# Three w_in blocks in four by seven products instead of eight, halves of w_in and w_out in turn, and an order from a planner

## The chip, the cores and the metric

The kernel runs on one core of one Trainium2 chip. The metric is the device time of one execution in microseconds (us); lower is better.

## What is computed

Attention with a soft cap on the scores, and behind it two feed-forward layers on the 896 tokens (batch 2 of 448, model width 768, inner width 2048). The reference, cut to what matters:

```
scores = cap * tanh(q @ k.T / 8 / cap)            # 2 x 12 heads, 448 x 448, head width 64
x  = softmax(scores) @ v                          # heads side by side: 896 x 768
h  = x @ w_in          # 768 -> 2048              first layer
x  = (s * relu(h)**2 + b) @ w_out                 # 2048 -> 768
h  = x @ w2_in         # 768 -> 2048              second layer
out = (h * clip(h + 3, 0, 6) / 6) @ w2_out        # 2048 -> 768
```

The four weight matrices reach the device as 64-bit words that hold each value in double format. The kernel makes float32 of them itself.

## The kernel before

**Precision.** Every float32 operand of a feed-forward product is split into two parts that TensorE multiplies in its fp32r format: `hi` is the value cast to fp32r, `lo` is the value minus `hi`. A product of a 128x128 weight block with a 128x448 operand block (448 tokens, one batch) is then three matmuls (lo·hi, hi·lo, hi·hi) into one PSUM bank. I call these three a piece. `products` (line 101) issues a piece.

**Tiling.** With KD = 6 blocks of 128 in the model width and KF = 16 in the inner width, each layer has 16 w_in chunks `f`, each of 6 pieces for each of the two batches (36 matmuls), and then 6 output blocks `mt`, each of 16 pieces for each batch, whose weights come in three chunks of 6, 6 and 4 blocks. That is 1152 matmuls a layer, 2304 in all, all recorded at line 104.

**A weight chunk's way.** SyncE's queue loads the raw 64-bit words of a chunk (`fetch`, line 54; up to 768 KB, three buffers `raw`). ScalarE rescales the upper halves (line 68). VectorE shifts them left by 3 (line 80), joins the sign bit (line 82) and joins the three top bits of the lower half (line 84). Then ScalarE casts `hi` (line 93) and VectorE subtracts `lo` (line 99).

**After the products.** `after_in` (line 106) makes the activation of a w_in chunk, once per batch: in the first layer Relu on ScalarE (110), square and scale on VectorE (114), `hi` on ScalarE (121), `lo` on VectorE (128). In the second layer VectorE has one instruction more (116, 117 and 130). `after_out` (132) splits the output into the next layer's operand, or copies it to `y` and stores it.

**Order.** In `iteration` (145) the code issues a piece and then one or more side steps of the chunks that come next (`beside`, 152), so order is what stands in the code: chunk after chunk, all 16 w_in chunks of a layer, then all of w_out.

**Attention.** It runs ahead of this, in 42 units of scores, tanh, exp and attend. Its last steps overlap with the first 18 pieces of the first layer (three chunks, first batch).

Of the kernel before, what the change touches and what calls it, by code (L numbers as in the profile page):

```python
# [9 lines left out]
U32 = mybir.dt.uint32  # L10
I32 = mybir.dt.int32
# [11 lines left out]
CH = 6  # L23
WARM = (S, S, S // 4)
SCALE = 1.0 / D**0.5
FIRST = 3


@with_exitstack
def attention_moe_moe(ctx: ExitStack, tc: tile.TileContext, qk, v, cap, w1i, w1o, s, b, w2i, w2o, out):  # L30
    nc = tc.nc
    const = ctx.enter_context(tc.tile_pool(name="const", bufs=1))
    act = ctx.enter_context(tc.tile_pool(name="act", bufs=1))
    wp = ctx.enter_context(tc.tile_pool(name="wp", bufs=3))
    tp = ctx.enter_context(tc.tile_pool(name="tp", bufs=4))
# [6 lines left out]
    zeros = tp.tile([128, S], F32, name="zeros", tag="h")  # L42
    ones = const.tile([128, D], F32, name="ones")
    x = [[act.tile([128, KD, S], F32R, name=f"x{p}{bi}") for p in ("h", "l")] for bi in range(B)]
    g = {(bi, f): [act.tile([128, S], F32R, name=f"g{p}{bi}{f}") for p in ("h", "l")] for bi in range(1) for f in range(FIRST)}

    chunks = [(w1i[f], 0, KD) for f in range(KF)]
    cuts = [(k, min(k + CH, KF)) for k in range(0, KF, CH)]
    chunks += [(w1o[m], *c) for m in range(KD) for c in cuts]
    chunks += [(w2i[f], 0, KD) for f in range(KF)]  # L50
    chunks += [(w2o[m], *c) for m in range(KD) for c in cuts]
    raws, whole, ready = {}, {}, {}

    def fetch(i):
        if i < len(chunks):
            src, k0, k1 = chunks[i]
            raws[i] = wp.tile([128, CH * 128, 2], U32, name="raw", tag="raw")
            nc.sync.dma_start(raws[i][:, :(k1 - k0) * 128, :], src[:, k0:k1, :].bitcast(U32).rearrange("p k (m t) -> p (k m) t", t=2))

    def rescale(i, dve=False):  # L60

        if i < len(chunks):
            n = (chunks[i][2] - chunks[i][1]) * 128
            up = raws[i][:, :n, 1].bitcast(F32)
            if dve:
                nc.vector.tensor_scalar(up, up, 2.0**-112, None, op0=ALU.mult)
            else:
                nc.scalar.activation(up, up, AF.Copy, scale=2.0**-112)  # L68

    def join(i, step):  # L70

        if i >= len(chunks):
            return
        n = (chunks[i][2] - chunks[i][1]) * 128
        if step == 0:
            whole[i] = wp.tile([128, CH * 128], F32, name="w", tag="w", bufs=2)
        bits = whole[i][:, :n].bitcast(U32)
        up, low = raws[i][:, :n, 1], raws[i][:, :n, 0]
        if step == 0:
            nc.vector.tensor_scalar(bits, up, 3, None, op0=ALU.logical_shift_left)  # L80
        elif step == 1:
            nc.vector.scalar_tensor_tensor(out=bits, in0=up, scalar=0x80000000, in1=bits, op0=ALU.bitwise_and, op1=ALU.bitwise_or)  # L82
        else:
            nc.vector.scalar_tensor_tensor(out=bits, in0=low, scalar=29, in1=bits,  # L84
                                           op0=ALU.logical_shift_right, op1=ALU.bitwise_or)
            raws.pop(i)
            fetch(i + 3)

    def upper(i, dve=False):
        if i < len(chunks):  # L90
            n = (chunks[i][2] - chunks[i][1]) * 128
            ready[i] = [wp.tile([128, CH * 128], F32R, name=f"w{p}", tag=f"w{p}") for p in ("hi", "lo")]
            (nc.vector.tensor_copy if dve else nc.scalar.copy)(ready[i][0][:, :n], whole[i][:, :n])  # L93

    def lower(i):
        if i < len(chunks):
            n = (chunks[i][2] - chunks[i][1]) * 128
            hi, lo = ready[i]
# [65 lines left out]
    def ffn():  # L164
# [23 lines left out]
        for _ in after:  # L188
            pass
# [256 lines left out]
```

## Time and profile before

| | |
|---|---|
| three runs | 566.32, 567.35, 575.05 us; median 567.35 |
| span of the profiled execution, first to last instruction | 565.5 us |
| TensorE busy in it | 559.1 us, 99% |
| VectorE, ScalarE busy in it | 376.9 us (67%), 261.3 us (46%) |

The span is the time that the profile's views divide up. A whole execution has a little more around it: the median run stands 1.85 us above the span, and the fastest 0.8 us. A time for the changed kernel is formed on the span, and the 1.85 us are added again.

### The profile page before, as it was taken

The page shows a single profiled execution, that of the slowest core. Times are in us where ns is not written, and L with a number is a line of the kernel's source. Part 1 is how long each engine was busy: PE and PEld are TensorE (multiplying, and loading weights), DVE is VectorE, ACT ScalarE, POOL GpSimd, SP SyncE. Part 2 cuts the span into 40 slices and gives each one's busy share as a digit, 9 for nine tenths or more (in the row PEclk, how much of TensorE's full clock was granted, in tenths as well). Part 3 has the DMA queues.
Part 4 walks back from the last instruction along what each step waited for, and adds up shares of the span by engine and source line. Part 5 has one row for each costly group of instructions (what it writes and reads, how often), then busy time and mean ns, then how long its engine had stood idle before and what let it go on. Part 6 is the DMA issues. An engine that isn't in the chain of part 4 may idle for free.

```text
span 565.5 us, 6988 instructions
## 1 busy us (share of the span) xinstructions
PE 559.1 (99%) x2790; PEld 459.5 (81%) x2790; DVE 376.9 (67%) x523; ACT 261.3 (46%) x376; POOL 0.4 (0%) x5
## 2 busy tenths in 40 slices
PE   8999999999999999999999999999999999999997
PEld 3223235799999999999999999999999999999996
DVE  2689887899777787545644568888888844544420
ACT  6999992455444443322222235544444532321210
POOL 0000000000000000000000000000000000000000
PEclk9999999999999999999999999999999999999999
DMA  8833411053333233224233413333332335333100
GB/s 318 311 123 121 147 35 34 0 165 115 112 114 111 94 111 119 81 100 150 93 94 112 168 56 112 111 112 111 113 111 83 105 134 159 125 126 127 55 33 34
DMA packets 15131, 64.13 MB, mean 113 GB/s; under 512 B 2022, under 2 KB 3962, under 8 KB 14970
## 3 DMA queue, kind: packets, MB, share of 16 engines
q1 hardware_dynamic: 14952, 63.52, 33.6%
q8 instruction: 22, 0.36, 0.3%
q10 hardware_dynamic: 146, 0.16, 0.1%
q14 instruction: 11, 0.09, 0.1%
HBM read 60.88 MB, written 2.79 MB: 113 GB/s over the span
## 4 chain that ended last, share of the span: by engine, by line
PE 95%; ACT 3%; issue 1%; DVE 1%
PE pf L104 82%; PE ps L222 5%; PE pav L248 4%; ACT t L230 2%; PE pav L245 1%; ACT t L235 1%; PE pz L267 1%; PE pz L336 1%; PE ps L226 1%; PE pz L275 1%; DVE xu L307 0%; DVE xl L312 0%; PE pz L293 0%; PE pz L290 0%; PE pf L290 0%
## 5 line engine op out<-in xcount | busy, mean ns | idle before, releaser
L104 PE MATMUL pf<-xh,wlo 128*128 128x448 f32 x384 | 140.7, 366 | 0.0
L104 PE MATMUL pf<-xl,whi 128*128 128x448 f32 x384 | 140.4, 366 | 0.3 <-DVE xl L312 0.3
L104 PE MATMUL pf<-xh,whi 128*128 128x448 f32 x384 | 140.3, 365 | 0.0
L104 PE MATMUL pf<-gl,whi 128*128 128x448 f32 x384 | 140.2, 365 | 0.0
L104 PE MATMUL pf<-gh,wlo 128*128 128x448 f32 x384 | 140.2, 365 | 0.0
L104 PE MATMUL pf<-gh,whi 128*128 128x448 f32 x384 | 140.2, 365 | 0.0
L93 ACT CAST whi<-w 128x768 fp32r<-128x768 f32 (+1 forms) x67 | 53.4, 797 | 166.3 <-PE pf L104 96.8
L99 DVE TENSOR_TENSOR wlo<-w,whi 128x768 fp32r<-128x768 f32 (+1 forms) x68 | 61.7, 907 | 83.7 <-ACT whi L93 83.7
L104 PEld LDWEIGHTS pf<-xh,wlo 128*128 128x128 f32 x384 | 72.1, 188 | 8.5 <-issue 2.1
L104 PEld LDWEIGHTS pf<-xl,whi 128*128 128x128 f32 x384 | 72.1, 188 | 6.4 <-DVE xl L312 0.7
L104 PEld LDWEIGHTS pf<-xh,whi 128*128 128x128 f32 x384 | 72.1, 188 | 5.7
L104 PEld LDWEIGHTS pf<-gl,whi 128*128 128x128 f32 x384 | 72.1, 188 | 5.7
L104 PEld LDWEIGHTS pf<-gh,wlo 128*128 128x128 f32 x384 | 72.1, 188 | 5.7
L104 PEld LDWEIGHTS pf<-gh,whi 128*128 128x128 f32 x384 | 72.1, 188 | 5.7
L82 DVE SCALAR_TENSOR_TENSOR w<-raw,w 128x768 uint32<-128x768 uint32 (+1 forms) x68 | 62.0, 912 | 2.2
L84 DVE SCALAR_TENSOR_TENSOR w<-raw,w 128x768 uint32<-128x768 uint32 (+1 forms) x68 | 61.9, 911 | 2.3
L68 ACT ACTIVATE raw<-raw 128x768 f32<-128x768 f32 (+1 forms) x67 | 58.1, 868 | 0.0
L230 ACT ACTIVATE t<-ps 128x896 f32<-128x896 f32 x42 | 37.9, 902 | 6.5 <-PE ps L222 6.5
L235 ACT ACTIVATE t<-t 128x896 f32<-128x896 f32 x42 | 39.9, 950 | 1.2
L80 DVE TENSOR_SCALAR w<-raw 128x768 uint32<-128x768 uint32 (+1 forms) x68 | 36.0, 530 | 0.0
L222 PE MATMUL ps<-rqk 64*128 64x448 f32 x144 | 34.8, 586 | 0.6 <-ACT t L230 0.5
L110 ACT ACTIVATE h<-pf,three 128x448 f32<-128x448 f32 x32 | 20.2, 632 | 27.9 <-PE pf L104 27.9
(56 smaller groups left out, 330.1 us busy)
## 6 DMA issues: line engine op xcount, KB each, us to landing
raw<-in_w1i SPq DMA_DIRECT2D x16, 768.0 KB, 4.1
raw<-in_w2i SPq DMA_DIRECT2D x16, 768.0 KB, 4.2
raw<-in_w1o SPq DMA_DIRECT2D x12, 768.0 KB, 4.1
raw<-in_w2o SPq DMA_DIRECT2D x12, 768.0 KB, 4.3
rqk<-in_qk SPq DMA_DIRECT2D x11, 448.0 KB, 6.0
raw<-in_w1o SPq DMA_DIRECT2D x6, 512.0 KB, 3.9
raw<-in_w2o SPq DMA_DIRECT2D x6, 512.0 KB
out<-y SPq DMA_DIRECT2D x12, 224.0 KB, 1.9
```

The costliest lines, as they stand in the source:

```text
L68: nc.scalar.activation(up, up, AF.Copy, scale=2.0**-112)
L80: nc.vector.tensor_scalar(bits, up, 3, None, op0=ALU.logical_shift_left)
L82: nc.vector.scalar_tensor_tensor(out=bits, in0=up, scalar=0x80000000, in1=bits, op0=ALU.bitwise_and, op1=ALU.bitwise_or)
L84: nc.vector.scalar_tensor_tensor(out=bits, in0=low, scalar=29, in1=bits, op0=ALU.logical_shift_right, op1=ALU.bitwise_or)
L93: (nc.vector.tensor_copy if dve else nc.scalar.copy)(ready[i][0][:, :n], whole[i][:, :n])
L99: nc.vector.tensor_sub(lo[:, :n], whole.pop(i)[:, :n], hi[:, :n].bitcast(F32))
L104: nc.tensor.matmul(ps[:, :S], w[a][:, sl], rhs[r], start=(k == 0 and i == 0), stop=(k == n_k - 1 and i == 2))
L110: nc.scalar.activation(t, ps[:, :S], AF.Relu, **({"bias": three} if layer else {}))
L222: nc.tensor.matmul(ps[:, j, :S], raw_qk[p][rows, 1, c * 128:(c + 1) * 128], raw_qk[p][rows, 0, :], start=True, stop=True)
L230: nc.scalar.activation(u_t[n], u_ps.pop(n)[:, :, :S], AF.Tanh, scale=icap_r)
L235: nc.scalar.activation(u_t[n], u_t[n], AF.Exp, scale=cap_r)
L248: nc.tensor.matmul(pav[p][(top, end)[j], :S], va[bi][:, d, (2 * (p % 2) + j) * NC + c, :], u_t[n][:, j, :], start=(p % 2 == 0 and c == 0), ...
```

## The change

It has five parts.

1. **Seven products.** Two w_in chunks `f`, `f+1` and the two batches are taken as a 2x2 block product (the 768 of the model width is cut in two, so each product is three pieces). Eight block products become seven by Strassen's method in a form with running sums. Seven operands are needed on either side: A11, A12, A22 and four sums S1 to S4 from the weights (VectorE, 128x384 each), B11, B21, B22 and four sums T1 to T4 from the layer's input. Partial results go from bank to bank: ScalarE copies product 1 into a second bank (`cp`) and product 5 into SBUF (`c5`); VectorE adds product 5 behind product 6 (`d1`) and behind product 7 (`d2`). The first 8 of the first layer's 16 chunks stay as they were (`PLAIN`), so 12 pairs of the 16 are done in this way.
2. **Halves.** Chunks 0 to 7 of w_in come first, then the 8 of the 16 inner blocks of all six output blocks, whose sums go to SBUF (`partial`); then chunks 8 to 15, and the second half of each output block on a bank that ScalarE has filled with the partial sum.
3. **Join on ScalarE.** The upper halves are rescaled into `w`; the three top bits of the lower half are shifted into the lowest byte of the upper half as bytes, by an ACTIVATE on every eighth byte (`low_bits`); VectorE then joins sign and low bits in one instruction (`merge`). For the first three chunks VectorE does the byte step.
4. **Planned order.** Every step of the feed-forward layers is a task with an engine, a cost and the buffers that it uses. `Plan.order` walks through time with these costs and takes, on each engine, the task that is due first and whose inputs and buffers are there; TensorE may take any of the next 36 pieces. The instructions are issued in the order of the planned starts.
5. **Buffers.** Activations and operands take slots of 128x448 (84 in all); weights lie in two groups of 4 blocks of 384 columns (`gA`) and two of 3 (`gB`).

```diff
-CH = 6
+HK = KD // 2
+BL = HK * 128
+CI = KD * 128
+HF = KF // 2
+CO = HF // 2 * 128
+PLAIN = 8
+SLOTS_A, SLOTS_B = 36, 48
+GROUPS = {"gA": 2, "gB": 2}
+OUT_ORDER = (0, 3, 1, 4, 2, 5)
...
-            nc.vector.tensor_scalar(bits, up, 3, None, op0=ALU.logical_shift_left)
-            nc.vector.scalar_tensor_tensor(out=bits, in0=up, scalar=0x80000000, in1=bits, op0=ALU.bitwise_and, op1=ALU.bitwise_or)
-            nc.vector.scalar_tensor_tensor(out=bits, in0=low, scalar=29, in1=bits,
-                                           op0=ALU.logical_shift_right, op1=ALU.bitwise_or)
...
+            nc.scalar.activation(by[:, :, 4], by[:, :, 3], AF.Copy, scale=1.0 / 32.0, bias=-15.5 / 32.0)
...
+        nc.vector.tensor_scalar(bits, bits, 3, None, op0=ALU.logical_shift_left)
...
+        nc.vector.scalar_tensor_tensor(out=bits, in0=up, scalar=0x80000007, in1=bits, op0=ALU.bitwise_and, op1=ALU.bitwise_or)
...
+            a = add("ACT", acts(n), hi, after, [g])
+            c = add("DVE", dve(n), lambda: nc.vector.tensor_sub(g.tile[1][:, at:at + n], cols, g.tile[0][:, at:at + n].bitcast(F32)), [a], [g])
...
+            s1 = add("DVE", dve(BL), lambda: nc.vector.tensor_add(blk(1), blk(4), blk(6)), [ms[1], *old])
+            s2 = add("DVE", dve(BL), lambda: nc.vector.tensor_sub(blk(3), blk(1), blk(0)), [ms[0], s1, *old])
+            s3 = add("DVE", dve(BL), lambda: nc.vector.tensor_sub(blk(5), blk(0), blk(4)), [*ms, *old])
+            s4 = add("DVE", dve(BL), lambda: nc.vector.tensor_sub(blk(7), blk(2), blk(3)), [ms[0], s2, *old])
...
+            ga, ta = parts("gA", flat[:, :4 * BL], 4 * BL, [ms[0], s1, s2], range(4))
+            gb, tb = parts("gB", flat[:, 5 * BL:], 3 * BL, [ms[1], s3, s4], (5, 6, 7))
...
+        def strassen(layer, f, w, ops):
+
+            a, bb, c = new_bank(), new_bank(), new_bank()
+            p1 = product(w["A11"], ops["B11"], a)
+            head = take_pe()
+            cp = add("ACT", acts(S), lambda: nc.scalar.copy(bb.tile[:, :S], a.tile[:, :S]), p1, [a, bb])
+            p5 = product(w["S1"], ops["T1"], c)
+            s5 = res("slot")
+            c5 = add("ACT", acts(S), lambda: nc.scalar.copy(t_of(s5, F32), c.tile[:, :S]), p5, [c, s5])
+            p2 = product(w["A12"], ops["B21"], a, [cp], first=False)
+            p6 = product(w["S2"], ops["T2"], bb, [cp], first=False, seeded=True)
+            mid = take_pe()
+            d1 = add("DVE", dve(S, True), lambda: nc.vector.tensor_add(c.tile[:, :S], bb.tile[:, :S], s5.tile), [*p6, c5], [bb, c, s5], 0.5)
+            p7 = product(w["S3"], ops["T3"], bb, [d1], first=False, seeded=True)
+            s7 = res("slot")
+            d2 = add("DVE", dve(S, True), lambda: nc.vector.tensor_add(t_of(s7, F32), bb.tile[:, :S], s5.tile), [*p7], [bb, s5, s7], 0.5)
+            p3 = product(w["S4"], ops["B22"], c, [d1], first=False)
+            p4 = product(w["A22"], ops["T4"], bb, [d2], first=False, seeded=True)
+            tail = take_pe()
...
+                head, mid, next_tail = strassen(layer, f, w, ops)
+                pe.extend(head + tail + mid)
+                tail = next_tail
+            pe.extend(tail)
```

In the order that the built programs have, VectorE's row of one w_in chunk in the first layer of the kernel before reads like this (`h` and `gl` are activations, `w` a weight chunk, `wlo` its lower part):

```order
L114 SCALAR_TENSOR_TENSOR h<-h,st 128x448 x2
L80 TENSOR_SCALAR w<-raw 128x768
L82 SCALAR_TENSOR_TENSOR w<-raw,w 128x768
L84 SCALAR_TENSOR_TENSOR w<-raw,w 128x768
L128 SCALAR_TENSOR_TENSOR gl_827<-h,bt,gh_826 128x448
L128 SCALAR_TENSOR_TENSOR gl_829<-h,bt,gh_828 128x448
L99 TENSOR_TENSOR wlo<-w,whi 128x768
```

That is one chunk: eight instructions (the first row holds two), in the same order for every chunk.

In the changed kernel VectorE's row in the first layer's pairs reads like this (`sl` is a slot; L626 is `d1`, L629 is `d2`, L520 to L523 are S1 to S4):

```order
L593 SCALAR_TENSOR_TENSOR sl<-sl,bt 128x448 x2
L579 SCALAR_TENSOR_TENSOR sl<-sl,st 128x448
L626 TENSOR_TENSOR pf<-pf,sl 128x448
L222 TENSOR_SCALAR w<-w 128x2x384 x2
L228 SCALAR_TENSOR_TENSOR w<-raw,w 128x2x384 x2
L629 TENSOR_TENSOR sl<-pf,sl 128x448
L520 TENSOR_TENSOR w<-w 128x384
L521 TENSOR_TENSOR w<-w 128x384
L522 TENSOR_TENSOR w<-w 128x384
L523 TENSOR_TENSOR w<-w 128x384
L593 SCALAR_TENSOR_TENSOR sl<-sl,bt 128x448
L579 SCALAR_TENSOR_TENSOR sl<-sl,st 128x448
```

One join step per chunk is gone, four sums per pair are new, and the two bank sums stand among the weight steps of the next pair.

On TensorE of the kernel before, a w_in chunk's second batch follows the first at once, on another bank, and no VectorE step lies between the two (bank `pf_2793` ends, `pf_2853` begins):

```order
L104 MATMUL pf_2793<-xh1_76,wlo_2720 128x448
L104 MATMUL pf_2793<-xl1_77,whi_2719 128x448
L104 MATMUL pf_2793<-xh1_76,whi_2719 128x448
L104 MATMUL pf_2853<-xh0_74,wlo_2781 128x448
L104 MATMUL pf_2853<-xl0_75,whi_2780 128x448
```

In both kernels each line is one matmul of a piece.

On TensorE of the changed kernel, between the first two pairs, product 6 of a pair ends on bank `pav_829`, product 1 of the next pair runs on `pz_830`, and then product 7 goes on upon `pav_829`:

```order
L232 MATMUL pav_829<-sl_1369,gAh_1561 128x448
L232 MATMUL pav_829<-sl_1316,gAh_1561 128x448
L232 MATMUL pz_830<-xh00_72,gAl_1735 128x448
L232 MATMUL pz_830<-xl00_73,gAh_1734 128x448
L232 MATMUL pz_830<-xh00_72,gAh_1734 128x448
L232 MATMUL pz_830<-xh01_74,gAl_1735 128x448
L232 MATMUL pz_830<-xl01_75,gAh_1734 128x448
L232 MATMUL pz_830<-xh01_74,gAh_1734 128x448
L232 MATMUL pz_830<-xh02_76,gAl_1735 128x448
L232 MATMUL pz_830<-xl02_77,gAh_1734 128x448
L232 MATMUL pz_830<-xh02_76,gAh_1734 128x448
L232 MATMUL pav_829<-sl_1383,gBl_1670 128x448
```

Nine matmuls of another product stand between product 6 and product 7, which needs `d1`. In the last pair of a half of the second layer no next pair is left. There the row of the changed kernel reads like this, product 6 with `gA` and product 7 with `gB`, both on bank `pf_760`:

```order
L232 MATMUL pf_760<-sl_2731,gAl_2965 128x448
L232 MATMUL pf_760<-sl_2748,gAh_2964 128x448
L232 MATMUL pf_760<-sl_2731,gAh_2964 128x448
L232 MATMUL pf_760<-sl_2402,gBl_3031 128x448
L232 MATMUL pf_760<-sl_2429,gBh_3030 128x448
```

Here product 7 follows product 6 with nothing between them.

## Rows read from the trace of the kernel before

**Rows 1.** Page, part 1: busy us of each engine, share of span, instructions.
```profile
PE 559.1 (99%) x2790; PEld 459.5 (81%) x2790; DVE 376.9 (67%) x523; ACT 261.3 (46%) x376; POOL 0.4 (0%) x5
```

**Rows 2.** Chain that ended last, in order of time: start us, us, what.
```profile
107.28 454.86 PE pf L104 x2243
...
562.16 0.53 ACT y L136
```

**Rows 3.** Instruction groups by form, first of six like groups: busy us, mean ns.
```profile
L104 PE MATMUL pf<-xh,wlo 128*128 128x448 f32 x384 | 140.7, 366 | 0.0
```

**Rows 4.** Stretches: us, PE, PEld, DVE, ACT, POOL busy (instructions), PEclk, DMA share, GB/s.
```profile
100.00:150.00 50.00, 49.69 (x244) 44.41 (x241) 44.24 (x62) 26.86 (x45) 0.00 (x0) 1.00 0.28 95
...
400.00:450.00 50.00, 50.00 (x248) 46.34 (x248) 42.83 (x71) 25.54 (x42) 0.00 (x0) 1.00 0.31 103
450.00:500.00 50.00, 50.00 (x249) 46.34 (x248) 24.78 (x34) 13.62 (x20) 0.00 (x0) 1.00 0.44 145
```

**Rows 5.** Page, part 2: granted TensorE clock in 40 slices, tenths of full speed.
```profile
PEclk9999999999999999999999999999999999999999
```

**Rows 6.** Groups by form, VectorE: busy us, mean ns of one.
```profile
L82 DVE SCALAR_TENSOR_TENSOR w<-raw,w 128x768 uint32<-128x768 uint32 x56 | 53.7, 959 | 1.8
...
L99 DVE TENSOR_TENSOR wlo<-w,whi 128x768 fp32r<-128x768 f32 x56 | 53.4, 953 | 65.5 <-ACT whi L93 65.5
...
L80 DVE TENSOR_SCALAR w<-raw 128x768 uint32<-128x768 uint32 x56 | 31.0, 553 | 0.0
L114 DVE SCALAR_TENSOR_TENSOR h<-h,st 128x448 f32<-128x448 f32 x32 | 21.3, 681 | 16.1 <-ACT h L110 16.1
L128 DVE SCALAR_TENSOR_TENSOR gl<-h,bt,gh 128x448 fp32r<-128x448 f32 x32 | 20.3, 678 | 0.0
...
L117 DVE TENSOR_TENSOR h<-pf,h 128x448 f32<-128x448 f32 x32 | 20.0, 625 | 1.1
...
L130 DVE TENSOR_TENSOR gl<-h,gh 128x448 fp32r<-128x448 f32 x32 | 18.5, 618 | 0.0
...
L116 DVE TENSOR_SCALAR h<-h 128x448 f32<-128x448 f32 x32 | 12.5, 390 | 14.8 <-ACT h L110 14.8
...
L99 DVE TENSOR_TENSOR wlo<-w,whi 128x512 fp32r<-128x512 f32 x12 | 8.3, 691 | 18.2 <-ACT whi L93 18.2
```

**Rows 7.** Groups by form, ScalarE: busy us, mean ns of one.
```profile
L68 ACT ACTIVATE raw<-raw 128x768 f32<-128x768 f32 x55 | 50.1, 910 | 0.0
L93 ACT CAST whi<-w 128x768 fp32r<-128x768 f32 x55 | 46.0, 837 | 155.9 <-PE pf L104 96.8 <-DVE w L84 59.0
...
L121 ACT ACTIVATE gh<-h,bt 128x448 fp32r<-128x448 f32 x32 | 19.5, 667 | 0.7 <-DVE h L114 0.7
...
L110 ACT ACTIVATE h<-pf 128x448 f32<-128x448 f32 x32 | 16.8, 541 | 24.9 <-PE pf L104 24.9
...
L93 ACT CAST whi<-w 128x512 fp32r<-128x512 f32 x12 | 7.4, 616 | 10.4 <-DVE w L84 10.4
```

**Rows 8.** VectorE in order of time, from 150 us: start us, us.
```profile
149.99 1.28 DVE L128 SCALAR_TENSOR_TENSOR gl<-h,bt,gh 128x448 fp32r<-128x448 f32 x2
151.19 0.95 DVE L99 TENSOR_TENSOR wlo<-w,whi 128x768 fp32r<-128x768 f32 x1
...
155.42 0.96 DVE L82 SCALAR_TENSOR_TENSOR w<-raw,w 128x768 uint32<-128x768 uint32 x1
156.42 0.96 DVE L84 SCALAR_TENSOR_TENSOR w<-raw,w 128x768 uint32<-128x768 uint32 x1
```

**Rows 9.** TensorE in order of time, around 107 us: a wait for VectorE ends.
```profile
107.28 0.47 PE L104 MATMUL pf<-xl,whi 128*128 128x448 f32 x1 [0.32 <-DVE xl L312]
...
107.59 0.36 PE L104 MATMUL pf<-xh,whi 128*128 128x448 f32 x1
```

**Rows 10.** DMA issues: KB each, median us from issue to landing.
```profile
raw<-in_w1i SPq DMA_DIRECT2D x16, 768.0 KB, 4.1
...
raw<-in_w1o SPq DMA_DIRECT2D x6, 512.0 KB, 3.9
```

More of the change, by code (lines that the diff above doesn't have):

```diff
@@ L10 @@
 U32 = mybir.dt.uint32
+U8 = mybir.dt.uint8
 I32 = mybir.dt.int32
@@ L26, with __init__ @@
 FIRST = 3
+PLAIN = 8
+SLOTS_A, SLOTS_B = 36, 48
+GROUPS = {"gA": 2, "gB": 2}
+OUT_ORDER = (0, 3, 1, 4, 2, 5)
+class Res:
+    def __init__(self, kind, tile=None):
+        self.kind, self.tile, self.left, self.held, self.order = kind, tile, 0, tile is not None, None
+class Task:
+    def __init__(self, engine, cost, run, after, use, number):
+        self.engine, self.cost, self.run, self.use, self.number = engine, cost, run, use, number
+        self.after = list(dict.fromkeys(t for t in after if t is not None))
+        self.then, self.due, self.start, self.end = [], 1e9, None, None
@@ L49, in attention_moe_moe @@
[L49 to L58, printed above, removed]
@@ L89, in upper @@
[L89 to L98, printed above, removed]
-            nc.vector.tensor_sub(lo[:, :n], whole.pop(i)[:, :n], hi[:, :n].bitcast(F32))
@@ L145, in iteration @@
-    def iteration(pieces, side):
-        for j, piece in enumerate(pieces):
-            piece()
-            for one in side[j * len(side) // len(pieces):(j + 1) * len(side) // len(pieces)]:
-                one()
-            yield
-    def beside(i, after):
-        return [lambda: next(after, None), lambda: rescale(i + 3), lambda: next(after, None),
-                lambda: join(i + 2, 0), lambda: join(i + 2, 1), lambda: join(i + 2, 2),
-                lambda: next(after, None), lambda: upper(i + 2), lambda: next(after, None), lambda: lower(i + 2)]
@@ L316, in finish_x, with w_src, early_region, early_fetch @@
         rest_x(p)
+    first_groups, raws = {}, {}
+    def w_src(layer, kind, i):
+        return ((w1i, w1o), (w2i, w2o))[layer][kind][i]
+    def early_region(i):
+        return flat[:, i * CI:(i + 1) * CI]
+    def early_fetch(i):
+        raws[i] = raw_tile()
+        load_raw(raws[i], w1i[i], CI)
+    def early_merge(i):
+        merge(raws[i], CI, early_region(i))
+        if i < FIRST:
+            raws.pop(i)
+            early_fetch(i + 3)
+    def early_upper(i, dve=False):
+        if i % 2 == 0:
+            first_groups[i // 2] = group("gA")
+        hi = first_groups[i // 2][0][:, i % 2 * CI:(i % 2 + 1) * CI]
+        (nc.vector.tensor_copy if dve else nc.scalar.copy)(hi, early_region(i))
@@ new lines, in early_lower, with early_w, first_pieces @@
+    def early_lower(i):
+        hi, lo = (t[:, i % 2 * CI:(i % 2 + 1) * CI] for t in first_groups[i // 2])
+        nc.vector.tensor_sub(lo, early_region(i), hi.bitcast(F32))
+    def early_w(i, k):
+        sl = slice(i % 2 * CI + k * 128, i % 2 * CI + (k + 1) * 128)
+        return [t[:, sl] for t in first_groups[i // 2]]
+    first_ps = []
+    def first_pieces():
+        for f in range(FIRST):
+            ps = psum()
+            first_ps.append(ps)
+            for k in range(KD):
+                matmuls(ps, early_w(f, k), x[0][k], k == 0, k == KD - 1)
+                yield
```

561 lines of the change are left out of this document (442 added, 119 removed).

## The prediction

> **What bounds the kernel now.** I read the page's busy shares first: TensorE is busy for 559.1 of 565.5 us [rows 1]. But a busy matmul here is one whose end is modelled: the groups give 365 to 366 ns for each of the six kinds of matmul [rows 3], and six times 140 us are more than the whole span, so they overlap. What a matmul costs must be read from the chain in order of time: from 107.28 us on it is one piece of 454.86 us with 2243 matmuls and nothing between them [rows 2]. That is 454.86 / 2243 = 0.2028 us for one. Behind it comes only a copy of 0.53 us and the last store. So the feed-forward part is bound by the number of its matmuls alone, and 108 fewer are worth what 108 cost, as long as the other engines keep up. Does a busier VectorE slow the matmuls? The stretches say no: with VectorE at 42.83 us of 50, TensorE starts 248 matmuls, with VectorE at 24.78 it starts 249 [rows 4]. The granted clock is full in every slice [rows 5].
>
> VectorE is the engine to watch: 44.24 us of 50 in the first stretch of the w_in stage [rows 4], 88%.
>
> **The matmuls.** A pair had 2 chunks x 36 = 72; with seven products of three pieces it has 63, and lasts 63 x 0.2028 = 12.8 us in place of 14.6. Twelve pairs save 12 x 9 = 108 matmuls, and the built program has indeed 2196 of them where 2304 stood. 108 x 0.2028 = 21.9 us. Attention, its first 18 pieces and the tail (copy, store) keep their order on every engine but for the join of three chunks, so they stay.
>
> **VectorE beside a pair.** From [rows 6], first layer, per pair: two shifts 2 x 0.553; two merges 2 x 0.958 (I take line 82's price, the same kind and size); S1 to S4 of 384 columns, which no row shows: from 512 and 768 columns (0.691, 0.953) one column costs 1.02 ns, so 0.56 each, 2.24; the lower parts of 1536 and 1152 columns by the same slope 1.74 + 1.35 = 3.09; d1 and d2, two inputs of which one is in PSUM, 2 x 0.625 (line 117); four activations 4 x (0.681 + 0.678) = 5.44. Sum 1.11 + 1.92 + 2.24 + 3.09 + 1.25 + 5.44 = 15.05 us beside 12.8 us of TensorE. In the second layer the activations cost 4 x (0.390 + 0.625 + 0.618) = 6.53, and the sum is 16.1. So VectorE doesn't fit beside a pair. It must borrow from the output blocks, where it has little to do: an output block has 48 matmuls, 9.7 us, and VectorE's two shifts (at most the 0.553 of 768 columns), two merges of 512 (0.69, as the other instruction of that size with two inputs) and one lower part of 1024 (0.691 + 512 x 0.00102 = 1.22) make at most 3.7 us. That is what the halves are for: over a half of the second layer (4 pairs, 6 blocks) VectorE has 4 x 16.1 + 6 x 3.7 = 87 us of work in 109.5 us. In the first layer's second half the new operands add 33 instructions of 0.62: 4 x 15.05 + 22 + 20.5 = 103 in 109.5. It fits if the planner can carry enough across the border. How much it carries I read from the order of the whole program: between the first and the last matmul of a run of four pairs (252 matmuls, 51.1 us) there stand 65 VectorE instructions in the first layer, worth 47.6 us by these rows, then 79 worth 50.9, then 76 worth 48.6. So VectorE is planned at 93 to 100% in three runs. Two things shift that. Instructions that don't need each other overlap: two of 0.68 took 1.20 up to the next start [rows 8], 0.08 less each. Those that do need each other leave 0.04 between them: 155.42 + 0.96, then 156.42 [rows 8]. Together the real need is a few per cent under the sums, so I take it that VectorE keeps up, but with no reserve.
>
> **Where TensorE waits.** Each pair has three hand-overs that the kernel before has not: `cp` (ScalarE) ahead of products 2 and 6, `d1` ahead of 7 and 3, `d2` ahead of 4. In the order nine matmuls, 1.8 us, stand between product 6 and product 7. The hand-over needs the tail of the last matmul (0.36 - 0.20 = 0.16), the sum (0.625), two crossings of 0.04, and the slower start of a matmul that waited (0.47 against 0.36 [rows 9]): 1.0 us. Covered, with 0.8 us to spare, if VectorE has nothing in front. Behind a late `d1` stand the next pair's shifts, merges and the conversion of its weights; TensorE waits for it. At two places, the last pair of each half of the second layer, nothing stands between product 6 and 7: 2 x 1.0 = 2.0 us on the path. For the other hand-overs I bound VectorE's lateness: at nothing, if the overlap above holds, and at 0.7 us for each of the 24 by `d1` and `d2` (two instructions of 0.62 to 0.96 in front, less what is spare), 16.8 us. I take 1.0 us, near the lower end, since the rows leave VectorE just below TensorE's pace. Waits at the output blocks for weights or activations have 7 or more matmuls of cover, most over 30, so nothing.
>
> **ScalarE beside a pair.** Two rescales 2 x 0.910, two byte steps, upper parts of 1536 and 1152 columns (0.86 ns a column from 512 and 768: 1.50 + 1.17), two copies 2 x 0.54, activations 4 x (0.541 + 0.667) [rows 7]. With 0.910 for a byte step, the nearest row (same count, same step of 8 bytes), that is 12.2 us beside 12.8. No row shows bytes: from below 0.837 (contiguous) or even less, from above I take twice the row, 1.82, which adds 1.8 us a pair and, spread over a run that needs 45 of 51 us, costs TensorE some 0 to 6 us in all. I take 0.910, no cost. The 48 copies of partial sums (0.54) stand in the output blocks, where ScalarE has room, and cost nothing.
>
> **Loads.** A half block's load of 512 KB lands 3.9 us after its issue [rows 10]; in the order some ten of 96 rescales stand only 16 to 18 matmuls (3.2 to 3.6 us) behind their issue. ScalarE waits up to 0.7 us there, ahead of weights that TensorE wants 9 matmuls later at the earliest: nothing on the path.
>
> **Sum.** 565.5 - 21.9 + 2.0 + 1.0 = 546.6 us of span; with the 1.85 us around it 548.5 us, 3.3% under the median of 567.35.
>
> **Rivals.** *A, VectorE is late at the hand-overs.* For it: 93 to 100% planned, and a queue in which `d1` stands behind weight steps. Against it: every wait of TensorE also gives VectorE time to catch up. By the upper bound 546.6 + 15.8 + 1.85 = 564 us, no change that can be told (a measurement tells about 2% here: 556.0 or 578.7).
>
> *B, the byte step costs double.* For it: no row has it. 548.5 + 4 = 552.5.
>
> *C, the borrowing fails.* Place: VectorE in the pairs, if groups of weights and slots come free so late that it can work ahead by nothing. Then a pair lasts as long as VectorE needs: 4 x (15.05 - 12.8) + 8 x (16.1 - 12.8) = 35 us, 567.35 - 21.9 + 35 = 580.5, slower. It eats the gain from an average of 1.8 us per pair on, and loses 2% from 2.8. Against it: the order's 47.6 to 50.9 us of VectorE per run.
>
> *D, the clock.* All slices show the full level of 2.4 GHz [rows 5], with pauses of TensorE of 0.32 us [rows 9]. If the new waits let it fall to 1.2 GHz for about one pair behind each of the two uncovered waits, that is 2 x 12.8 = 26 us: 574. The Trainium skill, "TensorE: Matmul & The Clock Gate", section "A second HAM failure mode: psum-queue depth-cycling", says that small idle times between groups of matmuls, where banks are cycled, made the clock swing; the trace of before has such a bank cycle, but no fall, and by that rule the sum would be D's.
>
> That the change doesn't save the matmuls is excluded by the count in the program.
>
> **Chances.** Forecast 0.70 (its own range 545.5, no wait at all, to 552); A 0.13; B 0.08; C 0.06; D 0.03. Faster by over 2%: 0.70 + 0.08 + a share of 0.03 of A (half of its price or less) = 0.81; same: the rest of A and D's part, 0.12; slower: C and a last 0.01, 0.07. The range for 8 in 10 begins at 544.5 (no waits, and 1 us from the shorter join in attention) and reaches up into A as far as 558.
>
> **What would show it.** The chain in time order should show the matmuls of line 232 at 0.203 us each, 2135 of them behind the end of attention, in pieces broken only by VectorE's line 626 at two places. The waits of TensorE for lines 626, 629 and 619 should sum to 2 to 4 us; 17 us would be A. Line 218 with 768 elements should read 0.84 to 0.95 us; 1.8 would be B. VectorE's busy time in a run of pairs should be 90% or more of it with TensorE still at 248 matmuls per 50 us. If a run of four pairs takes 60 us or more, C is right; a clock row below 1.00 is D. The attention part should end within 1 us of 107.

## The result, and the profile after

The changed kernel takes 557.38 us (median of 4, 556.39 to 560.48) beside 566.93 us for the kernel before in the same session (median of 4, 566.32 to 575.05): a ratio of 0.984, interval 0.980 to 0.9885. The prediction was 548.5. The direction is right, but 566.93 - 557.38 = 9.55 us came where 567.35 - 548.5 = 18.85 were forecast. The times of the kernel before cluster at two values, 566 to 567 and 575 to 576; the part on the matmuls' pace gives a reading of this.

The page of the changed kernel answers [rows 1] and [rows 5]: busy us of each engine, share of the span, instructions; then the granted clock in 40 slices.

```profile
span 556.4 us, 7002 instructions
...
PE 543.7 (98%) x2682; PEld 438.4 (79%) x2682; DVE 394.4 (71%) x587; ACT 423.6 (76%) x549; POOL 0.4 (0%) x5
...
PEclk9999999999999999999999999999999999999999
```

TensorE lost its 108 matmuls (2790 to 2682) and the clock is full. ScalarE is the surprise: 423.6 us where it had 261.3. It is now busier than VectorE, which the prediction took for the engine to watch. The span was forecast at 546.6 us and is 556.4, so 9.8 us are to be found.

The chain that ended last, in order of time (start us, us, what), answers [rows 2]:

```profile
158.72 1.35 ACT raw L218
161.98 15.26 PE pf L232 x74
...
223.13 3.59 ACT raw L218 x2
226.74 0.96 DVE w L228
...
308.47 19.84 PE pf L232 x96
...
414.95 9.72 PE pf L232 x48
...
537.83 14.89 PE pf L232 x72
```

Where one piece of 2243 matmuls stood, the chain now leaves TensorE again and again, mostly for line 218, the byte step on ScalarE. And the matmuls have two prices: 9.72 / 48 = 0.2025 us at 415 us, but 19.84 / 96 = 0.2067 at 308 us and 14.89 / 72 = 0.2068 at 538. Worked out from the starts of all line 232 matmuls behind 108.5 us: 21 gaps above 0.23 us hold 8.9 us more than 21 matmuls would, and the others follow each other at 0.2044 us on average (0.2027 before). So of the 9.8 us, 8.9 - 3.0 = 5.9 are waits beyond the 3.0 that were forecast, and 2128 x (0.2044 - 0.2028) = 3.4 are pace, as I call this spacing of matmuls that don't wait. The rest is in the last copy and store, and in rounding.

The waits of TensorE (engine, line, what it waited for; us in total, times, longest):

```profile
PE pf L232 <- ACT sl L587: 2.8, 1, 2.8
PE pf L232 <- DVE pz L626: 1.8, 2, 1.1
PE pf L232 <- DVE sl L593: 0.4, 1, 0.4
PE pav L232 <- DVE gAl L494: 0.3, 1, 0.3
PE pf L232 <- DVE sl L629: 0.2, 1, 0.2
PE pz L232 <- DVE sl L629: 0.2, 1, 0.2
```

This view counts only the engine's idle time. The gaps between starts also hold the tail of the matmul before and the slower start of the one that waited, so they sum to more (8.9 us). The two waits on line 626 (`d1`) are the uncovered hand-overs, forecast at 2 x 1.0. The one of 2.8 us, at the first output block, wasn't forecast. It stands at 161 us, ahead of the first pair by seven products, whose `cp` copy runs at 219 us. The groups by form (busy us, mean ns of one | idle before, releaser) show what is late; they answer [rows 6, 7]:

```profile
L218 ACT ACTIVATE raw<-raw 128x512 uint8<-128x512 uint8 x48 | 62.1, 1388 | 0.2
L218 ACT ACTIVATE raw<-raw 128x768 uint8<-128x768 uint8 x29 | 54.8, 1971 | 0.1
...
L228 DVE SCALAR_TENSOR_TENSOR w<-raw,w 128x512 uint32<-128x512 uint32 x48 | 33.0, 690 | 22.2 <-ACT raw L218 22.1
...
L228 DVE SCALAR_TENSOR_TENSOR w<-raw,w 128x768 uint32<-128x768 uint32 x32 | 30.7, 958 | 24.1 <-ACT raw L218 24.1
...
L494 DVE TENSOR_TENSOR gAl<-w,gAh 128x1536 fp32r<-128x1536 f32 x12 | 21.0, 1753 | 2.5 <-ACT gAh L492 2.5
...
L521 DVE TENSOR_TENSOR w<-w 128x384 f32<-128x384 f32 x12 | 6.7, 557 | 0.3
```

A byte step of 768 columns takes 1.97 us where 0.910 was priced and 1.82 was the upper bound; 512 columns take 1.39. The merges on VectorE wait 22.1 + 24.1 = 46.2 us for it. VectorE's own prices came out as worked out (0.557 for 0.56, 1.753 for 1.74, 0.958 for 0.958).

ScalarE in order of time, ahead of the wait of 2.8 us (start us, us, engine, line, operation):

```profile
153.21 1.35 ACT L218 ACTIVATE raw<-raw 128x512 uint8<-128x512 uint8 x1
...
155.03 1.37 ACT L218 ACTIVATE raw<-raw 128x512 uint8<-128x512 uint8 x1
...
158.72 1.34 ACT L218 ACTIVATE raw<-raw 128x512 uint8<-128x512 uint8 x1
...
160.34 0.66 ACT L587 ACTIVATE sl<-sl,bt 128x448 fp32r<-128x448 f32 x1
```

Line 587 makes the activations that the first output block reads. Byte steps of later output blocks stand in front of it, 1.1 us from one's start to what follows it, and TensorE is idle from 158.3 to 161.05 us.

### The profile page after: what moved, and what is told of

Read it like the earlier page. It is cut to its first block, busy times and chain, and to the rows that moved or that the text cites. A ratio compares the mean times of both kernels' runs of the same rounds, so it can differ in the third digit from the quotient of the medians.

```text
span 556.4 us, 7002 instructions
## 1 busy us (share of the span) xinstructions
PE 543.7 (98%) x2682; PEld 438.4 (79%) x2682; DVE 394.4 (71%) x587; ACT 423.6 (76%) x549; POOL 0.4 (0%) x5
## 4 chain that ended last, share of the span: by engine, by line
PE 71%; ACT 16%; DVE 9%; issue 3%
PE pf L232 31%; PE pav L232 20%; PE pz L232 7%; ACT raw L218 7%; PE ps L265 5%; PE pav L291 4%; ACT w L211 3%; DVE gBl L494 2%; DVE w L228 2%; ACT t L273 2%; ACT gAh L492 1%; PE pav L288 1%; DVE sl L579 1%; ACT t L278 1%; DVE sl L593 1%
## 5 line engine op out<-in xcount | busy, mean ns | idle before, releaser
L232 PE MATMUL pf<-sl,gBh 128*128 128x448 f32 x450 | 128.5, 367 | 0.4 <-DVE sl L593 0.4
L218 ACT ACTIVATE raw<-raw 128x512 uint8<-128x512 uint8 (+1 forms) x77 | 116.9, 1607 | 0.3
L228 DVE SCALAR_TENSOR_TENSOR w<-raw,w 128x512 uint32<-128x512 uint32 (+1 forms) x80 | 63.6, 798 | 46.3 <-ACT raw L218 46.2
L232 PEld LDWEIGHTS pf<-sl,gBh 128*128 128x128 f32 x450 | 84.4, 188 | 8.0 <-DVE sl L593 0.7
L232 PE MATMUL pf<-sl,gBl 128*128 128x448 f32 x225 | 83.0, 369 | 4.9 <-ACT sl L587 2.8
L232 PE MATMUL pav<-sl,gBh 128*128 128x448 f32 x238 | 68.0, 367 | 0.0
L211 ACT ACTIVATE w<-raw 128x512 f32<-128x512 f32 (+1 forms) x79 | 57.9, 763 | 7.6 <-DVE gBl L494 5.4
L232 PE MATMUL pf<-sl,gAh 128*128 128x448 f32 x198 | 56.6, 367 | 0.0
L232 PE MATMUL pav<-sl,gAh 128*128 128x448 f32 x172 | 49.0, 366 | 0.0
L232 PEld LDWEIGHTS pav<-sl,gBh 128*128 128x128 f32 x238 | 44.7, 188 | 4.0
```

The source lines that it names most:

```text
L211: nc.scalar.activation(bits, up, AF.Copy, scale=2.0**-112)
L218: nc.scalar.activation(by[:, :, 4], by[:, :, 3], AF.Copy, scale=1.0 / 32.0, bias=-15.5 / 32.0)
L232: nc.tensor.matmul(ps[:, :S], w[a], rhs[r], start=start and i == 0, stop=stop and i == 2, skip_group_check=True)
```

## Experiments

Theory 1: the byte step, twice as dear as priced, makes ScalarE hand operands over late. Theory 2, rival A of the prediction: VectorE is late at the hand-overs by itself. Theory 3: the rest is a pace of the matmuls that takes one of two values and is drawn anew where TensorE has waited. The sums of waits below are worked out as above, from the starts of the matmuls.

### The byte step made cheap

```
-            nc.scalar.activation(by[:, :, 4], by[:, :, 3], ...)
+            m = {768: 302, 512: 199}[n]
+            nc.scalar.activation(by[:, :m, 4], by[:, :m, 3], ...)
```

> The byte step on ScalarE (line 218) works on 302 of 768 and 199 of 512 columns, all else and the whole order unchanged; the low three bits of the other columns are left out of the weights. Theory 1 (the byte step took 1.39 and 1.97 us where 0.67 and 0.91 were planned, ScalarE ran late, and TensorE's waits of 9 us come from that): line 218 reads about 0.67 and 0.91 us, TensorE's waits fall to 2.5 to 4 us, the time to 548 to 552 us. Theory 2 (VectorE late at the hand-overs d1 and d2, whatever ScalarE does): waits stay at 8 us or more, time 555 to 558. Theory 3 (after a wait the matmuls can fall into a pace of 0.2067 us instead of 0.2027, by chance): with fewer waits fewer stretches at the slower pace, 0 to 4 us of difference between runs.

For the columns that the byte step no longer reaches, the kernel leaves out the low three bits of the weights. 554.42 us median (547.97 to 555.28, 6 runs), ratio 0.9785 [0.9766, 0.9804]; the profiled execution has a span of 547.4. Groups by form, and below them the waits of TensorE in the feed-forward part, line numbers one higher:

```profile
L219 ACT ACTIVATE raw<-raw 128x199 uint8<-128x199 uint8 x48 | 28.1, 680 | 0.2
L219 ACT ACTIVATE raw<-raw 128x302 uint8<-128x302 uint8 x29 | 24.2, 917 | 0.1
```

```profile
PE pf L233 <- DVE pz L627: 1.8, 2, 1.1
```

With the byte step at 0.917 us, the price of the prediction, and every instruction in the same order, only the two uncovered hand-overs are left; the sum of the waits is 2.4 us in place of 8.9. VectorE does the same work (393.0 us), so theory 2 is refuted: VectorE keeps up. ScalarE is busy for 363.9 us, so the dear byte step made up 60 of its 423.6.

In time, 547.97 and 549.18 are the predicted 548.5, but the four others lie about 6 us above. The median misses the 548 to 552 of theory 1, and the spread of 7.3 us the 0 to 4 of theory 3. The profile is of the execution of 549.18, and the granted clock was 0.999 to 1.000 in all six, so the clock isn't the reason; whether the four others lose their time by pace is not shown. By their times alone the two kernels can hardly be told apart (the ratio of the changed one is 0.984 [0.980, 0.9885]). What carries the reading is the waits in the profiles: the one of 2.8 us stands in all three that were taken of the changed kernel's program (one of them with instructions added behind it), and not in this one. The chain shows the output block that took 19.84 us above:

```profile
301.79 19.46 PE pf L233 x96
...
528.88 14.89 PE pf L233 x72
```

19.46 / 96 = 0.2027: the same work at the faster pace, while the end of this execution goes at 0.2068 too.

### What makes the byte step dear

Behind the last block, ten forms of it three times each on 448 columns, for instance:

```
+            nc.scalar.activation(by2[:, :, 4], by[:, :, 3], ...)   # L856
+            nc.scalar.activation(cont[:, :n], by[:, :, 3], ...)    # L858
+            nc.scalar.activation(fl, by[:, :, 3], ...)             # L864
+            nc.scalar.activation(by[:, :, 4], fl, ...)             # L866
```

> The changed kernel, with 30 more instructions behind its last output block, three of each form, on 448 columns: the byte step from and to every eighth byte, to contiguous bytes, from contiguous bytes, both contiguous, from every eighth byte to float32, from float32 to every eighth byte, on 16-bit halves with a step of 8 bytes; the byte and the 16-bit step on VectorE; the byte step on GpSimd. If reading bytes is slow on ScalarE, the forms that read bytes take about 1.25 us and float32 to bytes 0.57; if writing them is slow, bytes to float32 takes 0.57 and the others 1.25; if only the step of 8 bytes is, the contiguous form takes 0.57. On VectorE 1.042 us was seen for 768 columns, so 0.6 to 0.7 for 448. The body before it is a second profile of the changed kernel: theory 3 expects the slower pace in other stretches than in the first.

Groups by form in its last 37 us. The names read alike, so the text says by line which is which:

```profile
L866 ACT ACTIVATE raw<-mf 128x448 uint8<-128x448 f32 x3 | 3.6, 1194 | 0.1
L860 ACT ACTIVATE raw<-raw 128x448 uint8<-128x448 uint8 x3 | 3.6, 1193 | 0.1
L868 ACT ACTIVATE raw<-raw 128x448 uint16<-128x448 uint16 x3 | 3.6, 1193 | 0.1
L856 ACT ACTIVATE raw<-raw 128x448 uint8<-128x448 uint8 x3 | 3.6, 1193 | 7.0 <-DMA raw<-in_w1i 7.0
L874 POOL TENSOR_SCALAR raw<-raw 128x448 uint8<-128x448 uint8 x3 | 3.5, 1180 | 584.8 <-DVE raw L872 584.6
L870 DVE TENSOR_SCALAR raw<-raw 128x448 uint8<-128x448 uint8 x3 | 2.0, 664 | 53.0 <-ACT raw L868 52.9
...
L858 ACT ACTIVATE raw<-raw 128x448 uint8<-128x448 uint8 x3 | 1.8, 597 | 0.1
L864 ACT ACTIVATE mf<-raw 128x448 f32<-128x448 uint8 x3 | 1.8, 594 | 0.1
L862 ACT ACTIVATE raw<-raw 128x448 uint8<-128x448 uint8 x3 | 1.8, 590 | 0.1
```

Reading every eighth byte is free: into contiguous bytes 0.597 us (L858), into floats 0.594 (L864), against 0.590 with both sides contiguous (L862). Writing every eighth byte doubles the time, from bytes (L856, L860), from floats (L866), and with 16-bit elements (L868): the second of the three cases that were named. VectorE does the step in 0.664, GpSimd in 1.180. 16-bit elements without a step were not tried. What runs ahead of the last block is the changed kernel once more; the part on the pace comes back to its profile.

### The planner told the price

```
-            l = add("ACT", acts(n), lambda: low_bits(r.tile, n), ...)
+            l = add("ACT", 0.22 + 0.00228 * n, lambda: low_bits(r.tile, n), ...)
```

> Only a number of the planner is changed: the byte step's cost is 0.22 us + 2.28 ns a column, as measured, instead of 0.19 + 0.85; the work is the same, its order is planned anew. Theory 1: the planner moves the byte steps to where ScalarE has room, the waits fall from 9 us to 3 to 6, time 551 to 554. Theory 2: waits as before, time 556 to 558. If ScalarE has no room left at all, the waits stay but stand where the planner put them.

556.45 us (554.25 to 556.9), ratio 0.980 [0.977, 0.9835]: not to be told from the changed kernel. The waits sum to 7.3 us, and the longest, 1.2 us, is on line 619 of ScalarE:

```profile
PE pf L232 <- ACT pf L619: 2.3, 2, 1.2
```

Waits and time miss what theory 1 expected of this run (3 to 6 us, 551 to 554 us). The wait of 2.8 us is gone, but others came elsewhere: the new order spread the lateness and didn't remove it, which is the third outcome that was named. That ScalarE has no room for the step ahead of the merges fits this, but is not shown by it.

### All pairs by eight products

The pairs of strassen_run take the plain product of eight again; halves, byte join on ScalarE and planner stay.

> All 16 pairs by eight products (2304 matmuls), the other four parts of the change kept: halves, byte join on ScalarE, planner, buffers. Theory 1 and 2: 108 matmuls of 0.2028 us more are 21.9 us, the sums of Strassen's method and the hand-overs are gone, so both engines have room in most stretches; waits only in the first 60 us of the feed-forward part, 3 to 4 us: time 568 to 573, about the kernel before and a little over. If the waits came from the halves or the planner and not from the pairs, it would be 575 or more.

571.52 us median of 566.46, 566.84, 576.19 and 576.67. The kernel before had 566.14 to 567.34 and, twice, 575.55 and 575.96 in the same session, so the two are alike value by value. In the profile no matmul of the feed-forward part waits (no gap above 0.23 us) and all go at 0.2027. Its byte step is as dear (1.955 us for 768 columns, ScalarE 392.6 us busy). So the halves, the byte join and the planned order cost and bring nothing alone, and even the waits of 3 to 4 us that were expected in the first 60 us are absent: the waits need both the dear byte step and what the seven products add. That is not only the shorter pairs with their hand-overs. The waits at 117 and 161 us, 4.3 of the 8.9 us by the gaps, stand ahead of the first pair. There the changed kernel already makes the sums T1 to T4, with five casts of line 442 on ScalarE between 108 and 161 us (2.9 us), one of them right ahead of line 587, and this kernel makes none. Whether those casts alone bring the wait was not tried.

### The byte step on GpSimd, and product 6 first

```
-            nc.scalar.activation(by[:, :, 4], by[:, :, 3], ...)
+            nc.gpsimd.tensor_scalar(by[:, :, 4], by[:, :, 3], 1.0 / 32.0, -15.5 / 32.0, ...)
```

and in a second run, and alone in a third, product 6 ahead of product 2:

```
+            p6 = product(w["S2"], ops["T2"], bb, [cp], first=False, seeded=True)
             p2 = product(w["A12"], ops["B21"], a, [cp], first=False)
-            p6 = product(w["S2"], ops["T2"], bb, [cp], first=False, seeded=True)
```

> The byte step is moved from ScalarE to GpSimd (a multiply-add on the same bytes), and the planner is told its cost there. Theory 1 (ScalarE, slowed by the byte step that takes 1.97 us where 0.91 was priced, hands operands over late): ScalarE falls from 424 to about 300 us busy, the waits of TensorE in the feed-forward part shrink from 9 to 2 to 3 us, and only the two uncovered hand-overs on VectorE's sum d1 (1.8 us together) are left; 548 to 550 us where the matmuls go at 0.2027 us, 553 to 556 where a stretch of them goes at 0.2067. GpSimd's own price should be near 2.0 us for 768 columns (1.18 for 448), 150 us in all. Rival (VectorE is late at the hand-overs by itself): the waits named for VectorE stay, 555 to 558 us. A second rival: GpSimd beside VectorE slows VectorE's instructions; then the merges read more than 0.8 us and the time stays above 556.

> The byte step on GpSimd as in the run before it, and product 6 is asked for before product 2, so that nine matmuls of product 2 stand between product 6 and product 7 everywhere, also in the last pair of a half. If the two waits of 0.9 us on d1 are the uncovered hand-overs, they are gone: 1.8 us less than byte_pool at the same matmul pace, 546 to 548 us at 0.2027 us a matmul and 552 to 554 with a stretch at 0.2067. If the order of products was chosen so because of something else (bank or operand still in use), other waits of the same size take their place and the time is byte_pool's.

> The changed kernel with product 6 before product 2 alone; the byte step stays on ScalarE. Theory 1: the two waits on d1 go (1.8 us), the waits behind the late byte step stay (about 7 us): 554 to 557 us. If VectorE at the hand-overs is the main cause, covering product 7 takes away more than half of the 9 us of waits: 549 to 552.

The first took 595.53 us (ratio 1.051 [1.050, 1.053]), the second 589.64 (1.039 [1.037, 1.041]): far outside what theory 1 expected, by the second rival. Groups by form of the first; line 222, VectorE's shift, takes 423 and 557 ns in the changed kernel:

```profile
L222 DVE TENSOR_SCALAR w<-w 128x512 uint32<-128x512 uint32 x48 | 45.1, 962 | 13.4 <-ACT w L211 13.1
L222 DVE TENSOR_SCALAR w<-w 128x768 uint32<-128x768 uint32 x32 | 40.1, 1264 | 10.0 <-ACT w L211 9.8
```

While GpSimd works, VectorE's shift more than doubles: by the starts and ends in the trace, the 14 shifts of 512 columns that no GpSimd step overlaps take 0.41 us on average, the 34 others 1.19. VectorE's work grows to 469.8 us. So this edit slows another engine and can't speak for or against theory 1. Line 587 then comes 9.8 us late, and the stretches (us, PE, PEld, DVE, ACT, POOL busy, PEclk, DMA share, GB/s) show what this does to the clock:

```profile
155.00:160.00 5.00, 3.40 (x17) 2.81 (x15) 4.58 (x5) 2.40 (x5) 3.95 (x3) 1.00 0.00 0
160.00:165.00 5.00, 0.00 (x0) 0.00 (x0) 2.75 (x5) 2.60 (x4) 1.19 (x1) 0.68 0.68 210
165.00:170.00 5.00, 1.57 (x3) 1.08 (x4) 5.00 (x8) 2.63 (x6) 0.38 (x1) 0.50 0.48 137
170.00:175.00 5.00, 5.00 (x21) 4.52 (x21) 4.96 (x7) 2.11 (x4) 2.73 (x2) 0.80 0.19 76
175.00:180.00 5.00, 5.00 (x27) 4.64 (x26) 4.83 (x9) 2.62 (x4) 0.00 (x0) 1.00 0.54 166
```

The granted clock falls to 0.50, the lower level of 1.2 GHz, and the first whole 5 us behind the wait, from 170 us, hold 21 matmuls, the next 5 us 27.

Product 6 first, alone, gave 556.62 us (554.93 to 558.43), ratio 0.983 [0.980, 0.986], a time as theory 1 expected. The two waits on `d1` are gone as they should be, yet the sum of waits is 9.2 us, not 7: others of 0.5 to 0.7 us on lines 629, 593 and 619 took their place. The lateness moved to other hand-overs; what made those late was not traced. With the byte step on GpSimd the same reordering brought 5.9 us, where 1.8 were expected; why is open.

### Byte steps of w_out on VectorE

Three runs put byte steps of 512 columns on VectorE (0.767 us each) and keep product 6 first: those of layer 2 with the told cost, all 48 with the told cost, all 48 with the old cost.

```
-            l = add("ACT", acts(n), lambda: low_bits(r.tile, n), ...)
+            l = add("DVE" if dve_byte else "ACT", ..., lambda: low_bits(r.tile, n, dve_byte), ...)
```

> Three things at once: the byte step of the 24 w_out blocks of layer 2 on VectorE (a shift of bytes, by the row of 448 columns about 0.74 us for 512), the planner told the measured cost of the byte step on ScalarE (0.22 us plus 2.28 ns a column), and product 6 ahead of product 2. Theory 1 (ScalarE's slow byte step makes operands late): ScalarE loses 24 x 1.39 = 33 us, VectorE gains 18; the waits of TensorE in layer 2 should halve, from about 4 to 2 us, and the time is 2 to 4 us under the changed kernel: 553 to 556. Rival (VectorE has no reserve, so whatever is put on it comes back as a wait): waits named for VectorE grow, 557 to 562 us.

> As the run before it, but the byte step of all 48 w_out blocks on VectorE: ScalarE loses 67 us, VectorE gains 36. Theory 1: the waits behind ScalarE mostly go, and the time is 548 to 553 us. Rival: in the second half of layer 1 VectorE's work, 103 us in 109.5 by the prediction, passes the room it has (112), and about 3 us come back there: 553 to 557 us or more.

> The changed kernel with two edits: the byte step of the 48 w_out blocks on VectorE (it takes 36 us there, ScalarE loses 67), and product 6 ahead of product 2. The planner keeps its old cost of the byte step on ScalarE, so that it doesn't place two byte steps of 3.6 us together ahead of the copy that products 2 and 6 need, as at 350 us of the run with the told cost. Theory 1 (a byte step in front on ScalarE's queue makes operands late): the wait of 2.8 us at the first output block and that of 3.7 us at 350 us are both absent, TensorE's waits behind attention sum to 3 to 6 us in place of 9, and the time is 549 to 554 us. Rival (VectorE takes back what ScalarE gave): waits named for VectorE of 3 us or more in the second half of layer 1, and 555 us or more.

They took 557.22 us (ratio 0.983 [0.9775, 0.988]), 556.13 (0.980 [0.975, 0.985]) and 559.99 (0.988 [0.986, 0.990]). None is clearly faster than the changed kernel, and all three miss what theory 1 expected of them. The sums of waits are 8.3, 10.3 and 14.0 us (matmuls slowed behind a wait by a lower clock included), where 3 to 6 were expected of the last; in layer 2 they grew from 3.7 us in the changed kernel to 7.9 in the first run, where half was expected. The times are those of the rival, but the longest wait isn't: it is for ScalarE. The wait of 2.8 us at the first output block is gone in all three, but one of 3.7 us came up near 350 us, for line 619. ScalarE in order of time in the second run says why:

```profile
350.25 3.62 ACT L218 ACTIVATE raw<-raw 128x768 uint8<-128x768 uint8 x2
353.61 0.69 ACT L619 COPY pf<-pav 128x448 f32<-128x448 f32 x1
```

Two byte steps of w_in, 3.62 us, stand ahead of the copy `cp` that products 2 and 6 need. My expectation that the old cost would keep them apart was wrong; the same wait stands in the third run. In all three runs two w_in byte steps of together 3.6 us stand ahead of line 619 there. So these runs don't test theory 1 cleanly, and the cheap byte step stays its one clean test. The opposite split, w_in's byte steps on VectorE, was not tried.

### The matmuls' pace

Ten pauses were put into the kernel before, and the changed kernel was run once more as it is.

```
+    def gate(w, ps, i):
+        if i % 4 == 0:
+            nc.vector.scalar_tensor_tensor(out=w[0][:, :1], in0=ps[:, :1], scalar=0.0, in1=w[0][:, :1].bitcast(F32), ...)
```

> The kernel before with ten added waits of TensorE: in front of every fourth chunk VectorE rewrites one column of the weights from the bank of the chunk before (times zero), so that TensorE must pause until its last matmul has ended and VectorE has answered. Each pause should take 0.4 to 1.5 us, 4 to 15 us in all. Theory 3 (the spacing of matmuls takes one of two values, 0.2027 or 0.2067 us, and is drawn anew whenever TensorE has waited): some of the ten stretches, 2 to 6 of them, go at 0.2067 and the others at 0.2027, with changes only at the added waits; that adds 2 to 6 us. Rival (the slower spacing belongs to the seven products, their operands or their neighbours): every stretch goes at 0.2027.

> The changed kernel once more, unchanged. Theory 3: the waits stand at the same places (the sum of them is again 11 to 12 us with those of the attention's end), but which stretches go at 0.2067 us a matmul differs from the first profile, since it is drawn at each wait: 300 to 1300 of the 2130 matmuls. Rival (the pace belongs to places of the program): the same stretches, 220 to 229, 243 to 354 and 487 to 553 us.

The kernel before with pauses took 573.05 us (572.69 to 573.66), ratio 1.011 [1.010, 1.013]. Its chain from 214 us on:

```profile
213.96 77.91 PE pf L104 x383
...
292.19 54.60 PE pf L104 x263
...
435.80 53.55 PE pf L104 x263
```

Two stretches of 263 matmuls between two pauses differ by 1.05 us: 0.2076 each at 292 us, 0.2036 at 436 (both with the end of the last one), which is 0.004 for one. So the slower pace doesn't need the seven products. The slower pace is seen here in one of the stretches between pauses, fewer than the 2 to 6 that were expected.

In the changed kernel's second run (558.67 us, ratio 0.983 [0.979, 0.988]) the waits stand at the same places. The stretch from 243 to 355 us goes at 0.2067 again; the one behind the first output block is slow now and was fast, and the ones from 220 and from 488 us are fast now and were slow. So the pace is not a property of the place alone. But it isn't simply drawn at each wait either. The same program ran a third time in the kernel with the ten forms of the byte step behind it, and there the stretch from 243 us was slow once more. In all three it fell back to 0.2027 at the same place, 946 to 948 matmuls before the last, with no wait there. So slow stretches began where TensorE had waited, one of them ended without a wait, and theory 3 holds only in part; what decides the pace is open. The granted clock is 1.00 at both paces. If a whole feed-forward part went at 0.2067, the kernel before would take 2243 x 0.004 = 9.0 us longer, as its times of 575 to 576 do; no profile shows it there, so this stays a reading.

The second profile shows one thing more. Behind the same wait of 2.8 us the clock fell, which it had not done in the first. Stretches of the second execution:

```profile
155.00:160.00 5.00, 3.41 (x17) 2.82 (x15) 4.15 (x7) 4.94 (x8) 0.00 (x0) 1.00 0.81 229
160.00:165.00 5.00, 3.61 (x9) 2.85 (x10) 4.76 (x9) 5.00 (x10) 0.00 (x0) 0.60 0.51 185
165.00:170.00 5.00, 5.00 (x20) 4.51 (x19) 4.22 (x9) 3.15 (x4) 0.00 (x0) 0.72 0.38 110
```

and of the first:

```profile
160.00:165.00 5.00, 3.50 (x16) 3.01 (x17) 4.87 (x8) 5.00 (x10) 0.00 (x0) 1.00 0.55 168
165.00:170.00 5.00, 5.00 (x27) 4.63 (x26) 4.18 (x9) 3.08 (x5) 0.00 (x0) 1.00 0.45 122
```

Between 160 and 170 us TensorE started 29 matmuls with the clock at 0.60 and 0.72, and 43 with it at 1.00. By the gaps between starts this costs 2.4 us; the spans differ by 558.6 - 556.4 = 2.2. In the third execution, the kernel with the ten forms, the clock fell behind this wait too, to 0.75 between 160 and 165 us.

## Why the prediction was wrong, and what of it held

*The matmuls.* Right: 108 fewer, and at 0.2028 us they are worth 21.9 us; all of it shows in the count of the page.

*"108 fewer are worth what 108 cost, as long as the other engines keep up."* The matmul's price was taken as fixed, from a profile in which TensorE waits for nothing behind 107 us and keeps one pace throughout. In the changed kernel TensorE waits, and behind some of the waits its matmuls cost 0.2067. This term was put at nothing and measured 3.4 us; why the pace changes is open.

*VectorE beside a pair.* Right, against my own doubt and against rival A. The sum of 15.05 us per pair held to the row, and with a cheap byte step VectorE caused no wait but the two uncovered ones.

*Where TensorE waits.* The two uncovered hand-overs were forecast at 2.0 us with tail and slower start, and measured 2.4 by the gaps (1.8 as idle time alone). With the byte step at the price assumed they were all the waits there were, for a forecast of 3.0, so the 1.0 us for the other hand-overs by `d1` and `d2` wasn't needed. What failed stands in the paragraph's last sentence: waits at the output blocks were put at "nothing", for having 7 or more matmuls of cover. The first output block waited 2.8 us for its activations, since their cover counts TensorE's matmuls and not what stands in front on ScalarE.

*ScalarE beside a pair: "I take 0.910, no cost."* This is the step that failed, and the wait at the first output block hangs on it. The byte step takes 1.97 us for 768 columns and 1.39 for 512. The nearest row was one with the same count and the same step of 8 bytes, but it writes 4-byte elements; what doubles the time is to write narrow ones in steps, and no row of before did that. The upper bound, twice the row, was nearly right (1.82 for 1.97), but its cost was worked out by throughput, "some 0 to 6 us in all", from the pairs alone, with the output blocks taken as a place "where ScalarE has room". The need of 45 us in a run of four pairs isn't the paragraph's own sum either: 4 x 12.2 = 48.8 us of 51, and 56 with the bound. The extra waits measured 8.9 - 2.4 = 6.5 us, of which 4.3 stand ahead of the first pair, in a part that was not priced. So rival B was the right mechanism; it was given 4 us and a chance of 0.08.

*The range and the sign.* The measured 557.4 lies within the range for 8 in 10, 544.5 to 558, but by luck: the range reached that far for rival A's sake, and what filled it was the byte step and the pace. And the sign that was named for the waits, 2 to 4 us on lines 626, 629 and 619, came true with 1.8 + 0.4 = 2.2, while the long wait stood on line 587, which it didn't list. The sign on line 218 did tell: 1.97 us, and 1.8 was to mean B.

*Rivals.* A: refuted by the cheap byte step. B: right, 6.5 us for 4. C: it did not happen. In the stretch with most VectorE work TensorE still started 235 matmuls (answers [rows 4]), where pairs as long as VectorE's 16.1 us would allow 50 / 16.1 x 63 = 196:

```profile
450.00:500.00 50.00, 48.43 (x235) 43.69 (x234) 45.66 (x80) 43.04 (x66) 0.00 (x0) 1.00 0.27 85
```

D: not in the first profile of the changed kernel, but in small in the two others, in the second 2.4 us behind one wait. The Trainium skill's "TensorE: Matmul & The Clock Gate", section "A second HAM failure mode: psum-queue depth-cycling", would have let small idle times between groups do it; here the waits of 0.2 to 1.1 us left the clock at 1.00. It fell behind the wait of 2.8 us in two of three executions, and behind the one of 3.7 us in two of the three runs that had it.

*Sum.* 546.6 + 6.5 (byte step) + 3.4 (pace) - 0.6 (other waits, 2.4 for 3.0) = 555.9 us of span; measured 556.4.

## What to carry to other kernels

Before an edit puts a new form of instruction on an engine, look for a row that agrees with it in what it writes, not in how it reads or steps: width of the element and step of the output together set the price here. Price a dearer instruction by what stands behind it in its engine's queue at the tightest hand-over, not by the engine's mean load; ScalarE was 76% busy and still late. And a profile whose matmuls run without a pause need not show every price that they can have: it showed 0.2027 us here, and with pauses some stretches cost 0.2067.

## What the runs showed of the hardware

ScalarE writes 448 1-byte or 2-byte elements with a step of 8 bytes in 1.193 us, and contiguous bytes in 0.59; reading bytes in steps of 8 costs nothing. GpSimd at work on the same kind of step takes VectorE's shift of 512 columns from 423 to 962 ns on average, and only the shifts that it overlaps are slowed. The same matmul of 448 columns follows the one before in 0.2027 or in 0.2067 us over tens of microseconds at the same granted clock. And after one and the same wait of 2.8 us the granted clock fell in two executions and stayed in a third.
